# A transpose behind the last value product, a float32r sum over partitions and a last store in halves, in a fused attention and two-layer feed-forward kernel

## The chip, the cores and the metric

The kernel runs on one core of a Trainium2 chip. The metric is the device time of one execution in microseconds (us). Three timed executions of the kernel before took 597.98, 598.2 and 599.4 us, a median of 598.2 us.

## The reference

Causal attention over 2 batches, 12 heads, 448 positions and 64 channels; then a feed-forward layer with a leaky ReLU; then one with an RMS norm ahead and a gate:

```
attn = softmax(mask(q @ k.T / 8)) @ v             # 2 x 12 x 448 x 64
x    = attn, heads side by side                   # 896 x 768
h    = x @ w_in;  x = max(0.01*h, h) @ w_out      # 768 -> 2048 -> 768
rms  = sqrt(mean(x*x, axis=-1) + 1e-6)
xn   = x / rms * rms_g
g    = xn @ w_gate                                # 768 -> 1536
out  = (g*sigmoid(g) * (xn @ w_val)) @ w_out2     # 1536 -> 768
```

The weights and rms_g come as 64-bit floats and are decoded on the chip.

## The kernel before

Activations lie transposed, features on the 128 partitions and tokens in the free dimension, 448 per batch. Every large product is made of float32r operands in two parts, a high part (the value rounded to float32r) and a low part (what is left): high times high, low times high and high times low are accumulated in one PSUM bank, three matmuls of 128x448 where one would stand. The program has five stages on TensorE (PE).

1. **Attention**, some 97 us. A hand-written order (the string ORDER) interleaves 12 pairs of heads with the first weight pieces. A pair's probabilities are transposed on PE (line 365, plain float32 transposes against the identity `ident`), and its value product (line 385) multiplies them with v in plain float32, two heads side by side, each with 64 columns of weights. Steps y0 and y1 (lines 402 to 404) already compute two blocks of the first layer for batch 0. The last PE step of ORDER is x11, the last value product.
2. **First layer**: `first` (its `prod`, lines 152 to 154) does the same two blocks for batch 1, then 14 blocks at line 507 (36 matmuls each).
3. **Second product** (lines 523 to 525), six output blocks of 96 matmuls. ACT and DVE square each block and add the squares up in `ss`, 128 partitions by 896 tokens (lines 530 to 534).
4. **Gate and value products**, 12 blocks, each two weight pieces times two batches through `prod`, 18 matmuls each. In the first block, behind the gate product of each batch, `inv_rms` (line 541) sums `ss` over partitions: one plain float32 matmul of `ones` (128x128) with 448 columns (line 543). DVE and ACT make 1/rms of it (lines 545 to 552) and write it over `ss`; `gated` (line 558) multiplies it in.
5. **Last product** (lines 597 to 599), for two halves of 384 output columns, seven blocks of 128 tokens: 36 matmuls of 128x384 per block, a copy out of PSUM into `o`, on ACT for even blocks (line 608) and on DVE for odd ones (line 610), and a store of 192 KB issued by SP (line 611).

The weight pieces of stages 2 to 5 are loaded by SP and decoded by ACT and DVE (lines 103 to 139) one piece ahead of PE. PSUM is eight banks: four in the pool psS, three in psT (tag t, which the transposes of attention use too), one in psX; behind attention `bank()` hands them out in turn. Behind attention each engine's order is the order of a list scheduler, but for PE it is close to that of the code.

Of the kernel before, what the change touches and what calls it, by code (L numbers as in the profile page):

```python
# [6 lines left out]
F32 = mybir.dt.float32  # L7
F32R = mybir.dt.float32r
# [7 lines left out]
P = 128  # L16
B, H, S, D = 2, 12, 448, 64
# [3 lines left out]
Q = 64  # L21
T = B * S
# [49 lines left out]
def fused_kernel(tc, q, k, v, w_in, w_out, w_gate, w_val, w_out2, rms_g, out):  # L72
    nc = tc.nc
    PE, ACT, DVE, POOL, SP = nc.tensor, nc.scalar, nc.vector, nc.gpsimd, nc.sync

    with ExitStack() as top:
        const = top.enter_context(tc.tile_pool(name="const", bufs=1))
        wst = top.enter_context(tc.tile_pool(name="wst", bufs=2))
        slA = top.enter_context(tc.tile_pool(name="slA", bufs=1))
        mw = top.enter_context(tc.tile_pool(name="mw", bufs=2))  # L80

        ones = const.tile([P, P], F32, name="ones")
        POOL.memset(ones, 1.0)
        pace = const.tile([P, 2 * P], mybir.dt.bfloat16, name="pace")
        DVE.memset(pace, 1.0)
        rg = const.tile([P, KC], F32, name="rg")
# [59 lines left out]
        def rest(lo, x, hi, eng=None):  # L146
            (eng or DVE).tensor_tensor(out=lo, in0=x, in1=hi.bitcast(F32), op=ALU.subtract)
# [17 lines left out]
        HALF = DM // 2  # L165
# [24 lines left out]
        def piece(n, ahead=AHEAD):  # L190
            while len(ready) <= min(n + ahead, len(pieces) - 1):
                src, k_, m_, nm = pieces[len(ready)]
                hl = (None, None)
                if nm:
                    sl = slot(nm)
                    hl = (sl[:, 0, :k_ * m_], sl[:, 1, :k_ * m_])
                steps, parts = begun.pop(len(ready), None) or decode(src, k_, m_, *hl)
                for step in steps:
                    step()
                ready.append(parts())  # L200
            return ready[n]
# [35 lines left out]
        def attention(att, psS, psT, psX, ident, mask, mask_tail, keep_busy):  # L237
# [211 lines left out]
            for name in ORDER.split():  # L449
                name, _, eng = name.partition("@")  # L450
# [4 lines left out]
            assert all(name[0] == "l" and int(name[2:]) in PLAIN for name in do), do.keys()  # L455
            SP.dma_start(out=rg, in_=rms_g.rearrange("(c p) -> p c", p=P))
            ready.extend(L["w", f] for f in range(EARLY))

        psS = top.enter_context(tc.tile_pool(name="psS", bufs=4, space=PSUM))
        psT = top.enter_context(tc.tile_pool(name="psT", bufs=3, space=PSUM))  # L460
        psX = top.enter_context(tc.tile_pool(name="psX", bufs=1, space=PSUM))
        with tc.manual_schedule(), tc.tile_pool(name="att", bufs=2) as att:
            ident = att.tile([P, P], F32, name="ident", bufs=1)
            make_identity(nc, ident)
            mask = att.tile([P, 3 * P], F32, name="mask", bufs=1)
            mask_tail = att.tile([P, S], F32, name="mask_tail", bufs=1)
            for t, rows in ((mask, P), (mask_tail, Q)):
                POOL.memset(t, 0.0)
                for lo in range(0, P, rows):
                    tri = t[lo:lo + rows, -rows:]  # L470
                    POOL.affine_select(out=tri, in_=tri, pattern=[[-1, rows]], compare_op=ALU.is_ge, fill=-BIG,
                                       base=0, channel_multiplier=1)

            warm = psX.tile([P, 512], F32, tag="x", name="warm")

            def keep_busy(n):
                for _ in range(n):
                    PE.matmul(warm[:, :2 * P], pace[:, :P], pace, start=True, stop=True)

            keep_busy(14)  # L480
            attention(att, psS, psT, psX, ident, mask, mask_tail, keep_busy)
# [4 lines left out]
        mx = top.enter_context(tc.tile_pool(name="mx", bufs=2))  # L486
# [3 lines left out]
        def bank(n=S):  # L490
            pool, tag = ((psT, "t"), (psT, "t"), (psT, "t"), (psS, "s"),
                         (psS, "s"), (psS, "s"), (psS, "s"), (psX, "x"))[cnt[0] % 8]
            cnt[0] += 1
            return pool.tile([P, 512], F32, tag=tag, name="mm")[:, :n]
# [6 lines left out]
        for f in range(EARLY, NF1):  # L501
            wt, pss = piece(f), [bank() for _ in range(B)]
            for kk in range(KC):
                wh, wl = wt[kk]
                for w, part in ((wh, 0), (wh, 1), (wl, 0)):
                    for b in range(B):
                        PE.matmul(pss[b], w, cols(xT[kk], b)[part], start=kk + part == 0 and w is wh,  # L507
                                  stop=kk == KC - 1 and w is wl)
# [6 lines left out]
        ss = one.tile([P, T], F32, name="ss")  # L515
        for m in range(KC):
# [9 lines left out]
            for b in range(B):  # L526
                ps = pss[b]
                sq = ss[:, b * S:(b + 1) * S]
# [10 lines left out]


        def inv_rms(b):
            ps = bank()
            PE.matmul(ps, ones, ss[:, b * S:(b + 1) * S], start=True, stop=True)
            ms = mx.tile([P, S], F32, tag="t0", name="ms")
            DVE.tensor_scalar(out=ms, in0=ps, scalar1=1.0 / DM, scalar2=1e-6, op0=ALU.mult, op1=ALU.add)
            r0 = mw.tile([P, S], F32, tag="t1", name="r0")
            ACT.activation(out=r0, in_=ms, func=AF.Abs_reciprocal_sqrt)

            e = mx.tile([P, S], F32, tag="t2", name="e")
            ACT.activation(out=e, in_=r0, func=AF.Square)  # L550
            DVE.scalar_tensor_tensor(out=e, in0=e, scalar=-0.5, in1=ms, op0=ALU.mult, op1=ALU.mult)
            DVE.scalar_tensor_tensor(out=ss[:, b * S:(b + 1) * S], in0=e, scalar=1.5, in1=r0,
                                     op0=ALU.add, op1=ALU.mult)
# [17 lines left out]
        for f in range(NF2):  # L571
            banks = [[None] * B, [None] * B]
            for half in range(2):
                wt = piece(at_gate[f, half])
                for b in range(B):
                    ps = banks[half][b] = bank()
                    prod(ps, [(wt[kk], cols(x2[kk], b)) for kk in range(KC)])
                    if f == 0 and half == 0:
                        inv_rms(b)
                    if half:  # L580
                        gated(f, b, banks[0][b], ps)


        for nh in range(2):
            w2 = []
            for i in range(6):
                w2 += piece(at_w2[nh, i], 0)
            open_ = {}

            def rows(t, lo, hi):  # L590
                if t not in open_:
                    open_[t] = bank(HALF)
                ps = open_[t]
                for f in range(lo, hi):
                    th = tT[f][:, 0, t * P:(t + 1) * P]
                    tl = tT[f][:, 1, t * P:(t + 1) * P]
                    PE.matmul(ps, th, w2[f][0], start=(f == 0), stop=False)  # L597
                    PE.matmul(ps, th, w2[f][1], start=False, stop=False)  # L598
                    PE.matmul(ps, tl, w2[f][0], start=False, stop=(f == NF2 - 1))  # L599

            rows(0, 0, 8)
            rows(1, 0, 8)
            for t in range(T // P):
                rows(t, 8 if t < 2 else 0, NF2)
                ps = open_[t]
                o = mx.tile([P, HALF], F32, tag="t0", name="o")
                if t % 2 == 0:
                    ACT.copy(out=o, in_=ps)
                else:
                    DVE.tensor_copy(out=o, in_=ps)  # L610
                SP.dma_start(out=out[t * P:(t + 1) * P, nh * HALF:(nh + 1) * HALF], in_=o)


# [28 lines left out]
```

## Time and profile before

| | |
|---|---|
| the three timed executions | 597.98, 598.2, 599.4 us; median 598.2 |
| the profiled execution | 597.57 us |
| its span, first to last instruction | 595.7 us |
| PE busy | 588.1 us of the span (99%) |
| DVE, ACT, POOL busy | 386.3 (65%), 264.1 (44%), 48.2 us (8%) |
| attention / stages 2 and 3 with the first gate product / rest of 4 / stage 5 | to 97.4 / to 331.8 / to 504.8 / to 595.7 us |

The profiled execution lies 0.63 us below the median of the timed ones. The time outside its span is 597.57 - 595.7 = 1.9 us. In the profile a matmul's duration is longer than the distance to the next one's start, since matmuls are pipelined: what counts for PE's time is the distance from start to start. A plain float32 matmul is recorded as two, a float32r one or a transpose as one.

### The profile page before, as it was taken

To read this page: it belongs to the slowest core of one execution; us is meant where nothing else is said; L and a number is where in the kernel's file an instruction comes from. 1 tells how busy PE (TensorE), PEld (TensorE's weight loads), DVE (VectorE), ACT (ScalarE), POOL (GpSimd) and SP (SyncE) were. 2 spreads that over 40 slices of the span, in tenths; PEclk is the share of its full clock that TensorE was granted. 3 is DMA by queue.
4 is the path that set the end of the run, shared out by engine and by line. 5 is a ranking of instruction groups with operands and counts; after the bars stand their busy time and mean duration, and the time that the engine had idled before them with its cause. 6 is when DMAs were issued, how large, how long until landed. Compare 5 with 4: busy or idle time off the path is not lost.

```text
span 595.7 us, 8511 instructions
## 1 busy us (share of the span) xinstructions
PE 588.1 (99%) x3266; PEld 532.3 (89%) x3266; DVE 386.3 (65%) x704; ACT 264.1 (44%) x516; POOL 48.2 (8%) x105
## 2 busy tenths in 40 slices
PE   8999999999999999999999999999999999999997
PEld 5778877999999999999999899999999999999997
DVE  4989986866666555555655898797797796850000
ACT  5989883444444434323432753443444444320000
POOL 3644650000000000000000000000000000000000
PEclk9999999999999999999999999999999999999999
DMA  5575451533333323323333334343353352621001
GB/s 130 119 164 115 95 153 45 168 111 107 107 104 105 107 94 116 106 90 114 116 106 107 107 125 140 106 160 111 110 157 120 120 145 88 185 80 41 28 26 41
DMA packets 83992, 65.04 MB, mean 109 GB/s; under 512 B 36080, under 2 KB 80880, under 8 KB 83952
## 3 DMA queue, kind: packets, MB, share of 16 engines
q1 hardware_dynamic: 83024, 64.27, 36.7%
q8 instruction: 26, 0.43, 0.3%
q10 hardware_dynamic: 928, 0.23, 0.2%
q14 instruction: 14, 0.11, 0.1%
HBM read 61.74 MB, written 2.75 MB: 108 GB/s over the span
## 4 chain that ended last, share of the span: by engine, by line
PE 94%; POOL 1%; ACT 1%; DMA 1%; SPq 1%; DVE 1%; issue 0%; POOLq 0%; ACTq 0%; DVEq 0%
PE mm L507 17%; PE mm L152 10%; PE mm L153 10%; PE mm L154 10%; PE mm L524 7%; PE mm L525 7%; PE mm L523 7%; PE mm L599 5%; PE mm L598 5%; PE mm L597 5%; PE s L328 3%; PE pt L365 3%; PE x L385 3%; PE qk L288 1%; POOL p L358 1%; ACT p L345 1%
## 5 line engine op out<-in xcount | busy, mean ns | idle before, releaser
L152 PE MATMUL mm<-a,hi 128*128 128x448 f32 x300 | 110.4, 368 | 0.0
L154 PE MATMUL mm<-a,hi 128*128 128x448 f32 x300 | 109.6, 365 | 0.0
L153 PE MATMUL mm<-a,lo 128*128 128x448 f32 x300 | 109.6, 365 | 0.0
L133 ACT CAST hi<-we 128x768 fp32r<-128x768 f32 (+1 forms) x58 | 47.2, 815 | 137.1 <-PE mm L507 53.6
L139 DVE TENSOR_TENSOR lo<-we,hi 128x768 fp32r<-128x768 f32 (+1 forms) x60 | 55.8, 929 | 66.2 <-ACT hi L133 66.0
L122 DVE SCALAR_TENSOR_TENSOR we<-we,ws 128x768 int32<-128x768 int32 (+1 forms) x70 | 65.6, 937 | 28.9 <-ACT we L111 26.9
L507 PE MATMUL mm<-a,hi 128*128 128x448 f32 x336 | 83.0, 368 | 0.0
L111 ACT ACTIVATE we<-raw 128x768 f32<-128x768 f32 (+1 forms) x67 | 59.5, 888 | 38.1 <-DVE lo L139 24.3
L507 PEld LDWEIGHTS mm<-a,hi 128*128 128x128 f32 x336 | 63.1, 188 | 6.3
L126 DVE SCALAR_TENSOR_TENSOR we<-raw,we 128x768 int32<-128x768 int32 (+1 forms) x70 | 65.3, 933 | 1.4
L523 PE MATMUL mm<-b,hi 128*128 128x448 f32 x168 | 61.8, 368 | 0.0
L524 PE MATMUL mm<-b,hi 128*128 128x448 f32 x168 | 61.8, 368 | 0.0
L525 PE MATMUL mm<-b,lo 128*128 128x448 f32 x168 | 61.8, 368 | 0.0
L152 PEld LDWEIGHTS mm<-a,hi 128*128 128x128 f32 x300 | 56.4, 188 | 4.9 <-issue 0.4
L153 PEld LDWEIGHTS mm<-a,lo 128*128 128x128 f32 x300 | 56.4, 188 | 4.9 <-issue 0.4
L154 PEld LDWEIGHTS mm<-a,hi 128*128 128x128 f32 x300 | 56.4, 188 | 4.5
L507 PE MATMUL mm<-a,lo 128*128 128x448 f32 x168 | 48.3, 368 | 0.0
L345 ACT ACTIVATE p<-p,st 128x128 f32<-128x128 f32 (+3 forms) x84 | 44.0, 531 | 2.7 <-DVE st L336 2.5
L118 DVE TENSOR_SCALAR ws<-raw 128x768 int32<-128x768 uint32 (+1 forms) x70 | 37.9, 542 | 5.2 <-DMA raw<-in_moe_w_out_dram 2.6
L358 POOL TENSOR_SCALAR p<-p,st 128x384 f32<-128x384 f32 (+3 forms) x76 | 38.5, 528 | 30.0 <-DVE st L354 19.0
L610 DVE COPY o<-mm 128x384 f32<-128x384 f32 x6 | 3.3, 556 | 53.2 <-PE mm L599 53.2
L523 PEld LDWEIGHTS mm<-b,hi 128*128 128x128 f32 x168 | 31.6, 188 | 3.2
(125 smaller groups left out, 931.7 us busy)
## 6 DMA issues: line engine op xcount, KB each, us to landing
raw<-in_moe_w_out_dram SPq DMA_DIRECT2D x24, 768.0 KB, 4.3
raw<-in_moe_w_in_dram SPq DMA_DIRECT2D x16, 768.0 KB, 4.7
raw<-in_moe_w_gate_dram SPq DMA_DIRECT2D x12, 768.0 KB, 4.3
raw<-in_moe_w_val_dram SPq DMA_DIRECT2D x12, 768.0 KB, 4.3
raw<-in_moe_w_out_dram SPq DMA_DIRECT2D x6, 512.0 KB, 3.4
n<-in_k_dram SPq DMA_DIRECT2D x24, 112.0 KB, 2.8
out_dram<-o SPq DMA_DIRECT2D x14, 192.0 KB, 1.9
vn<-in_v_dram SPq DMA_DIRECT2D x24, 96.0 KB, 2.4
```

Source lines behind the costliest of these rows:

```text
L111: ACT.activation(out=out, in_=src, func=AF.Copy, scale=2.0 ** -112)
L122: DVE.scalar_tensor_tensor(out=L["e"], in0=L["e"], scalar=3, in1=L["s"], op0=ALU.logical_shift_left, op1=ALU.bitwise_or)
L126: DVE.scalar_tensor_tensor(out=L["e"], in0=L["w"][:, :, 1], scalar=-0x80000000, in1=L["e"], op0=ALU.bitwise_and, op1=ALU.bitwise_or)
L139: DVE.tensor_tensor(out=L["lo"], in0=L["e"].bitcast(F32), in1=L["hi"].bitcast(F32), op=ALU.subtract)
L152: PE.matmul(ps, wh, ah, start=(i == 0), stop=False)
L153: PE.matmul(ps, wl, ah, start=False, stop=False)
L154: PE.matmul(ps, wh, al, start=False, stop=(i == n - 1))
L345: ACT.activation(out=pr, in_=pr, func=AF.Exp, scale=-1.0, bias=st[:, 0, m:m + 1], accum_out=st[:, 1, m:m + 1])
L507: PE.matmul(pss[b], w, cols(xT[kk], b)[part], start=kk + part == 0 and w is wh, stop=kk == KC - 1 and w is wl)
L523: PE.matmul(pss[b], wh, ah, start=(f == 0), stop=False)
L524: PE.matmul(pss[b], wh, al, start=False, stop=False)
L525: PE.matmul(pss[b], wl, ah, start=False, stop=(f == NF1 - 1))
```

## The change

Three edits. `ones` becomes a float32r tile, so that `inv_rms` can split `ss` into a high part `sh` (copied by ACT) and a low part `sl` (subtracted on DVE, through `rest`, line 147) and accumulate two float32r matmuls in place of a plain float32 one. Behind the whole of ORDER stands one transpose of 64 rows of the identity into a fresh psT bank, whose result nobody reads. The last of the 14 output blocks is copied and stored in two halves of 192 columns: ACT copies and stores the first, DVE copies the second and SP stores it.

```diff
-        ones = const.tile([P, P], F32, name="ones")
-        POOL.memset(ones, 1.0)
+        ones = const.tile([P, P], F32R, name="ones")
+        POOL.memset(ones.bitcast(F32), 1.0)
...
             ready.extend(L["w", f] for f in range(EARLY))
+            PE.transpose(psT.tile([P, 512], F32, tag="t", name="pt")[:, :Q], ident[:Q], ident[:Q, :Q])
...
         def inv_rms(b):
-            ps = bank()
-            PE.matmul(ps, ones, ss[:, b * S:(b + 1) * S], start=True, stop=True)
+            ps, sq = bank(), ss[:, b * S:(b + 1) * S]
+            sh = mw.tile([P, S], F32R, tag="t1", name="sh")
+            ACT.copy(out=sh, in_=sq)
+            sl = mx.tile([P, S], F32R, tag="t2", name="sl")
+            rest(sl, sq, sh)
+            PE.matmul(ps, ones, sh, start=True, stop=False)
+            PE.matmul(ps, ones, sl, start=False, stop=True)
...
                 o = mx.tile([P, HALF], F32, tag="t0", name="o")
-                if t % 2 == 0:
-                    ACT.copy(out=o, in_=ps)
-                else:
-                    DVE.tensor_copy(out=o, in_=ps)
-                SP.dma_start(out=out[t * P:(t + 1) * P, nh * HALF:(nh + 1) * HALF], in_=o)
+                cuts = [0, HALF // 2, HALF] if (nh, t) == (1, T // P - 1) else [0, HALF]
+                for i, (lo, hi) in enumerate(zip(cuts, cuts[1:])):
+                    if (t + i) % 2 == 0:
+                        ACT.copy(out=o[:, lo:hi], in_=ps[:, lo:hi])
+                    else:
+                        DVE.tensor_copy(out=o[:, lo:hi], in_=ps[:, lo:hi])
+                    (ACT if i == 0 and len(cuts) > 2 else SP).dma_start(
+                        out=out[t * P:(t + 1) * P, nh * HALF + lo:nh * HALF + hi], in_=o[:, lo:hi])
```

The order of the instructions on PE at the end of attention, as one piece of the difference (x is the value product's bank, pt the transpose's, mm a bank of the first layer, a_72 the first slice of attention's output, hi and lo the parts of a weight piece):

```order
 L385 MATMUL x<-pT,vn_129 64x192 x2
 L385 MATMUL x<-pT,vn_129 64x64 x2
+L458 MATMUL pt<-ident 128x64
 L152 MATMUL mm<-a_72,hi 128x448
 L153 MATMUL mm<-a_72,lo 128x448
```

Nothing moved here but the added transpose, which stands between the last value product and the first float32r matmul of stage 2.

PE at the first `inv_rms`, in stage 4, with the semaphores that a row waits for (each is named for the engine that counts it up, or for a DMA queue), before:

```order
L154 MATMUL mm<-a_2462,hi 128x448 [waits DVE_49]
L543 MATMUL mm<-ss,ones 128x448
L152 MATMUL mm<-a_2457,hi 128x448
L153 MATMUL mm<-a_2457,lo 128x448
L154 MATMUL mm<-a_2457,hi 128x448
```

and with the change:

```order
L154 MATMUL mm<-a_2464,hi 128x448 [waits DVE_49]
L548 MATMUL mm<-sh,ones 128x448 [waits Activation_49]
L152 MATMUL mm<-a_2459,hi 128x448
L549 MATMUL mm<-sl,ones 128x448 [waits DVE_49]
L153 MATMUL mm<-a_2459,lo 128x448
L154 MATMUL mm<-a_2459,hi 128x448
```

The two new matmuls wait, one for ACT and one for DVE, and the next product's first matmul stands between them. DVE at the same place with the change (lo, we and ws belong to the decoding of a weight piece; L551 reads the sum):

```order
L538 SCALAR_TENSOR_TENSOR a_2464<-mm,rg,a_2464 128x448 [waits Activation_49]
L139 TENSOR_TENSOR lo<-we,hi 128x768 [waits PE_49,Activation_49]
L147 TENSOR_TENSOR sl<-ss,sh 128x448 [waits Activation_49]
L122 SCALAR_TENSOR_TENSOR we<-we,ws 128x768 [waits Activation_49]
L551 TENSOR_SCALAR ms<-mm 128x448 [waits PE_49]
```

The low part sl stands behind a weight piece's L139; on ACT its high part sh (L545) stands behind that piece's L133 and ahead of the next piece's L111.

DVE at the end of the program with the change:

```order
L618 COPY o<-mm 128x384 [waits DMAHW4_49,DVE_49,PE_49]
L618 COPY o<-mm 128x384 [waits DMAHW3_49,DMAHW5_49,DMAHW0_49,DMAHW7_49,PE_49,Activation_49]
L618 COPY o<-mm 128x384 [waits DMAHW1_49,DVE_49,PE_49]
L618 COPY o<-mm 128x384 [waits DMAHW3_49,DVE_49,PE_49]
L618 COPY o<-mm 128x192 [waits DMAHW4_49,DMAHW2_49,DMAHW6_49,DMAHW0_49,Activation_49]
```

The added half copy waits for ACT, not for PE: the ACT instruction that it waits for is the copy of the first half, which writes the same tile and reads the same bank.

## Rows read from the trace of the kernel before

**Rows 1.** The page: granted clock by slice, and the chain that ended last.

```profile
PEclk9999999999999999999999999999999999999999
PE 94%; POOL 1%; ACT 1%; DMA 1%; SPq 1%; DVE 1%; issue 0%; POOLq 0%; ACTq 0%; DVEq 0%
```

**Rows 2.** Two stretches: us, PE busy (matmuls) and other engines, clock, DMA.

```profile
97.70:331.84 234.14, 234.14 (x1134) 212.68 (x1133) 141.85 (x194) 92.84 (x152) 0.00 (x0) 1.00 0.35 112
337.20:504.80 167.60, 167.60 (x829) 155.35 (x828) 139.21 (x203) 74.52 (x105) 0.00 (x0) 1.00 0.41 126
```

**Rows 3.** Timeline of PE, end of attention: start us, us, engine, line, operation.

```profile
96.84 0.61 PE L385 MATMUL x<-pT,vn 128*64 128x192 f32 x8
97.38 0.47 PE L152 MATMUL mm<-a,hi 128*128 128x448 f32 x1
97.70 0.36 PE L153 MATMUL mm<-a,lo 128*128 128x448 f32 x1
```

**Rows 4.** Timeline of PE, float32r behind transposes (qk is one's bank).

```profile
70.73 0.27 PE L291 MATMUL qk<-ident,end 128*128 128x128 f32 x1
70.76 0.45 PE L402 MATMUL mm<-a,hi 128*128 128x448 f32 x1
71.05 0.37 PE L403 MATMUL mm<-a,lo 128*128 128x448 f32 x1
...
72.67 0.38 PE L365 MATMUL pt<-ident,p 128*128 128x128 f32 x2
```

**Rows 5.** Timeline, both `inv_rms` on PE: the float32 matmul, the second row behind it.

```profile
331.84 0.92 PE L543 MATMUL mm<-ss,ones 128*128 128x448 f32 x2
...
332.80 0.37 PE L153 MATMUL mm<-a,lo 128*128 128x448 f32 x1
...
336.25 0.91 PE L543 MATMUL mm<-ss,ones 128*128 128x448 f32 x2
...
337.20 0.36 PE L153 MATMUL mm<-a,lo 128*128 128x448 f32 x1
```

**Rows 6.** Timeline, ACT and DVE ahead of the first `inv_rms`.

```profile
329.60 0.85 ACT L133 CAST hi<-we 128x768 fp32r<-128x768 f32 x1
...
330.57 0.94 DVE L139 TENSOR_TENSOR lo<-we,hi 128x768 fp32r<-128x768 f32 x1
...
332.47 0.96 DVE L122 SCALAR_TENSOR_TENSOR we<-we,ws 128x768 int32<-128x768 int32 x1 [0.97 <-ACT we L111]
```

**Rows 7.** Groups by line and shape: busy us, mean ns of one, idle before.

```profile
L378 ACT COPY pT<-pt 128x512 f32<-128x512 f32 x38 | 21.5, 582 | 4.8 <-PE pt L365 4.3
...
L147 DVE TENSOR_TENSOR b<-g,b 128x448 fp32r<-128x448 f32 x28 | 16.3, 622 | 4.8 <-ACT b L219 4.8
...
L219 ACT CAST b<-g 128x448 fp32r<-128x448 f32 x28 | 14.4, 571 | 0.0
...
L378 DVE COPY pT<-pt 128x512 f32<-128x512 f32 x10 | 6.8, 685 | 0.7 <-PE pt L365 0.6
...
L608 ACT COPY o<-mm 128x384 f32<-128x384 f32 x8 | 3.8, 479 | 62.0 <-PE mm L599 62.0
...
L610 DVE COPY o<-mm 128x384 f32<-128x384 f32 x6 | 3.3, 556 | 53.2 <-PE mm L599 53.2
```

**Rows 8.** Timeline, end of the program.

```profile
592.43 0.48 ACT L608 COPY o<-mm 128x384 f32<-128x384 f32 x1 [12.01 <-PE mm L599]
592.93 0.33 SPq L611 DMA_DIRECT2D out_dram<-o  x1
```

**Rows 9.** DMA issues: count, KB each, median us to landing.

```profile
out_dram<-o SPq DMA_DIRECT2D x14, 192.0 KB, 1.9
vn<-in_v_dram SPq DMA_DIRECT2D x24, 96.0 KB, 2.4
...
vn<-in_v_dram SPq DMA_DIRECT2D x12, 32.0 KB, 2.4
```

**Rows 10.** Waits: who waited for whom, us in total, times, longest.

```profile
ACT hi L133 <- PE mm L507: 53.6, 14, 4.2
```

## The prediction

> **What bounds the kernel.** I read the page first: the chain that ended last is PE for 94% of the span, and the granted clock is full in every slice, the 2.4 GHz level [rows 1]. Behind attention nothing else ends a wait for long, so the time there is a number of matmuls times the distance from one start to the next. The second view, busy time by stretch, gives that distance, and it is not the same everywhere [rows 2]. From 97.70 to 331.84 us PE is never idle and starts 1133 matmuls of 128x448 (the row counts one more, still in flight at its left edge): 234.14 / 1133 = 0.2067 us each. From 337.20 to 504.80 us it starts 827 of the same shape and type (the row counts one in flight at either edge): 167.60 / 827 = 0.2027 us. The clock is 1.00 in both, the lines of `prod` stand in both, and neither has idle time. The same form runs 4.0 ns slower in the first stretch than in the second.
>
> The third view, PE's timeline, shows what stands at the borders. The slow stretch begins straight behind the last value product, whose matmuls use 64 columns of weights in pairs [rows 3]. It ends at the plain float32 matmul of `inv_rms` [rows 5]: the gate product's first 18 matmuls ahead of it still go at 0.2067, those behind it at 0.2027. A third place decides: in attention a run of eight float32r matmuls of 128x448, entered from transposes, takes from 71.05 to 72.67 us [rows 4]. That is 1.62 / 8 = 0.2025 us, where the slow pace would need 1.65. So I read the pace as something that PE keeps from how it entered a run of float32r matmuls: slow out of the value product, fast out of a transpose or a 128-column float32 matmul.
>
> **The transpose.** It stands exactly at the slow entry. If it acts as the transposes of rows 4 do, all 1133 distances fall to 0.2027: 1133 x 0.0040 = 4.53 us off PE, which is the path. Nothing behind it has to keep up that does not already: ACT's high part of the next weight piece waited for PE in 14 of the 14 blocks of line 507, 3.8 us a time [rows 10], and a block of 36 matmuls shortens by only 0.14. Its own cost: in rows 4 the float32r matmul starts 0.03 us behind the last transpose and the next one 0.29 behind that, against 0.32 between the first two in rows 3. That makes it nothing at the least and about 0.1 at the most; I take +0.05. Its bank is an extra turn in psT, free since the last transposes.
>
> **The sum over partitions.** From the start of the float32 matmul to the start of the second row behind it are 0.96 and 0.95 us [rows 5]. One of the 0.2027 in it belongs to the float32r matmul, so each sum costs 0.75. Now it is two float32r matmuls, 2 x 0.2027 = 0.41, and 0.34 is saved, twice: -0.69. The new operands are covered, but barely. ACT makes sh (571 ns for a cast of this width, rows 7) behind the high part that ends at 330.45, so by 331.02 [rows 6]. DVE makes sl (622 ns) behind L139, which ends at 331.51, so at 332.13, inside an idle 0.97 us. PE, at the fast pace behind the second product, comes to the sl matmul at 331.84 - 22 x 0.004 + 2 x 0.203 = 332.16. The scheduler's extra matmul between the two gives just this much, so I add +0.05 for a wait. Behind the wait stands the rest of the second batch's product. At the second sum I count no wait of its own; one of this size is within the range. What ACT and DVE do later for it (two casts and two subtractions, 2.4 us in all) lies beside the 36 value matmuls that follow, 36 x 0.2027 = 7.3 us.
>
> **The last store.** This looks like a saving and the order says it is not. Before, ACT's copy starts at 592.43 and SP issues 0.50 us later [rows 8]. Now DVE's half waits for ACT's half. From 384 to 512 columns ACT's copies grow from 479 to 582 ns and DVE's from 556 to 685 [rows 7], so 192 columns take some 325 and 362 ns: 0.325 + 0.03 + 0.362 + 0.02 = 0.74, and the last issue comes 0.24 us later. What the half as large store gives back is not in the trace: loads of 96 and of 32 KB both land after 2.4 us, so nothing; in proportion to bytes, half of 1.9, 0.95 [rows 9]. So between -0.71 and +0.24. The loads are the nearer rows, as they change the size alone, but the stores go the other way; I take 0.14 back and +0.10 for the edit.
>
> **The sum.** -4.53 + 0.05 - 0.69 + 0.05 + 0.10 = -5.02 us: 597.57 - 5.0 = 592.6 us for the profiled execution. The median of the runs shown lies 0.63 above it, so I forecast 593.2 us, 0.84% less. A measurement of this kernel can tell about 0.3%, 1.8 us, from no change.
>
> **Rivals**, each on the same scale (598.2 before).
>
> The pace outlives the transpose. The added one covers only 64 of the 128 rows, while every transpose that I see ahead of fast runs covers 112 or 128. If it leaves the slow pace standing, the change takes away the only thing that ended it, the float32 matmul: the two float32r matmuls are of the form that runs in either pace, and the 846 gate and value matmuls behind the first sum go at 0.2067 too. That is +3.38, with -0.68 for the sums and +0.2 for the rest: 601.1 us, slower; up to 2.0 more if the last stage's 504 matmuls, which ran at 173 ns each, were slower as well by 4 ns. It decides at one point: whether the second start behind the transpose lies 0.203 or 0.207 behind the first, and stays there. For it: the difference in rows. Against it: the entry is then from another instruction than a value product.
>
> The pace belongs to the stage and not to its entry, to something in operands or buffers of the first stretch that I don't see. Then the transpose does nothing and the gate stage stays fast: -0.69 + 0.2 = -0.5, 597.7 us. Against it speaks that `prod` runs at both paces on the same operands on either side of the sum. [...]
>
> The transpose helps, and the wait at the sl matmul enters the run anew and slowly. Then 3.38 is given back: -4.53 + 3.38 - 0.68 + 0.2 = -1.6, 596.6 us.
>
> **Chances.** Fast throughout, 593.2 us: 0.74. Slow throughout, 601.1: 0.11. No effect of the transpose, 597.7: 0.09. Half given back, 596.6: 0.06. Faster by over 0.3% (below 596.4) is the first case alone, 0.74; within 0.3% are the two small savings, 0.15; slower 0.11. The range begins at 592.0: the forecast less the best end of the store, 0.8, and the uncertainty of the median. It must reach the half-way case to hold eight in ten, so it ends at 596.8; the likeliest case alone lies within 592.0 and 594.0.
>
> **What would show it.** Right: behind 97.7 us the 1133 float32r matmuls take 229.6 us instead of 234.1; the gate stage keeps 0.2027; the two sums take 0.41 us each with no wait above 0.1; the last issue comes 0.74 us behind the start of ACT's copy and DVE's copy starts as ACT's ends. Wrong: a distance of 0.2067 behind the transpose, or behind 332 us; a sum that costs 0.7 because PE stood for sl; DVE's and ACT's half copies side by side.

## The result, and the profile after

The changed kernel took 593.1 us (median of four executions, 592.66 to 593.52) beside 598.13 us for the kernel before on the same chip: ratio 0.9911, 95% interval 0.9894 to 0.9928. The forecast was 593.2. The profiled execution took 592.95 us.

First the page: the span with its instructions, the busy times, and the chain that ended last.

```profile
span 591.2 us, 8521 instructions
...
PE 584.7 (99%) x3267; PEld 534.0 (90%) x3267; DVE 387.6 (66%) x707; ACT 265.2 (45%) x518; POOL 48.3 (8%) x105
...
PE 95%; POOL 1%; ACT 1%; DVE 1%; DMA 1%; issue 0%; ACTq 0%; POOLq 0%
```

Nothing here tells what happened: PE bounds the kernel as before [rows 1] and is 99% busy as before. The stretches do, in the columns of [rows 2].

```profile
98.34:327.96 229.62, 229.62 (x1134) 212.78 (x1133) 141.78 (x195) 93.24 (x153) 0.00 (x0) 1.00 0.37 114
333.75:500.30 166.55, 166.55 (x823) 154.34 (x822) 139.23 (x203) 74.54 (x104) 0.00 (x0) 1.00 0.41 126
```

The first stretch holds the same 1133 distances as in [rows 2]. They took 234.14 us and now take 229.62: 0.2027 us each in place of 0.2067. The second stretch keeps its pace (166.55 / 0.2027 = 822 distances). The clock is 1.00 in both. PE's timeline at the entry, with the transpose in the first row:

```profile
97.83 0.27 PE L458 MATMUL pt<-ident 64*128 64x64 f32 x1
98.04 0.47 PE L152 MATMUL mm<-a,hi 128*128 128x448 f32 x1
98.34 0.36 PE L153 MATMUL mm<-a,lo 128*128 128x448 f32 x1
```

The rows are rounded to 0.01 us; by the trace's nanoseconds the first float32r matmul starts 201 ns behind the transpose, and the second 306 ns behind the first, close to the 313 ns of [rows 3]. PE at the first sum:

```profile
327.96 0.36 PE L548 MATMUL mm<-sh,ones 128*128 128x448 f32 x1
328.16 0.37 PE L152 MATMUL mm<-a,hi 128*128 128x448 f32 x1
328.37 0.47 PE L549 MATMUL mm<-sl,ones 128*128 128x448 f32 x1
328.69 0.37 PE L153 MATMUL mm<-a,lo 128*128 128x448 f32 x1
```

ACT and DVE there, and the weight load of the sl matmul (PEld is the part of PE that loads weights ahead of a matmul):

```profile
326.53 0.60 ACT L545 CAST sh<-ss 128x448 fp32r<-128x448 f32 x1
...
327.70 0.62 DVE L147 TENSOR_TENSOR sl<-ss,sh 128x448 fp32r<-128x448 f32 x1
...
328.37 0.19 PEld L549 LDWEIGHTS mm<-sl,ones 128*128 128x128 f32 x1 [0.22 <-DVE sl L147]
```

DVE's low part ends at 328.32, and the weight load of the sl matmul, for which PEld stood idle for 0.22 us, starts at 328.37 together with the matmul. The matmul itself comes almost in time, but it takes 0.11 us longer than its neighbours (0.47 instead of 0.36) and the next start lies 0.31 behind it instead of 0.20. The whole sum costs 0.41 + 0.11, against 0.75 for the float32 matmul that it replaces. The end of the program, in the order of time:

```profile
587.53 0.34 PE L605 MATMUL mm<-hi,b 128*128 128x384 f32 x1
...
587.95 0.32 ACT L616 COPY o<-mm 128x192 f32<-128x192 f32 x1 [12.01 <-PE mm L605]
...
588.30 0.37 ACTq L619 DMA_DIRECT2D out_dram<-o  x1
588.30 0.36 DVE L618 COPY o<-mm 128x192 f32<-128x192 f32 x1 [6.08 <-ACT o L616]
588.69 0.33 SPq L619 DMA_DIRECT2D out_dram<-o  x1
```

The DMA issues to the output (count, KB each, median us to landing):

```profile
out_dram<-o SPq DMA_DIRECT2D x13, 192.0 KB, 1.9
out_dram<-o ACTq DMA_DIRECT2D x1, 96.0 KB, 1.7
out_dram<-o SPq DMA_DIRECT2D x1, 96.0 KB, 1.6
```

DVE's half copy starts as ACT's ends. The last issue stands 0.74 us behind the start of ACT's copy (before 0.50, rows 8), and the halves land in 1.7 and 1.6 us instead of 1.9.

Where the span's 4.52 us went (595.69 to 591.17; starts of the same instructions in both traces, in nanoseconds and then rounded):

| part | before | after | difference | forecast |
|---|---|---|---|---|
| up to the last value product (nothing changed there) | 95.50 | 95.95 | +0.45 | 0 |
| value product to the first float32r matmul | 1.88 | 2.08 | +0.20 | +0.05 |
| the first distance behind it | 0.31 | 0.31 | -0.01 | 0 |
| 1133 distances | 234.15 | 229.62 | -4.53 | -4.53 |
| first sum to the last product | 172.95 | 172.38 | -0.57 | -0.64 |
| last product to its last matmul | 87.21 | 87.19 | -0.02 | 0 |
| last matmul to the end | 3.68 | 3.63 | -0.05 | +0.10 |

Without the first row, in which the programs do not differ, -4.97 us stand against the -5.02 of the sum.

### The profile page after: what moved, and what is told of

The parts are those of the page before. It is cut to its first block, busy times and chain, and to the rows that moved or that the text cites. A ratio compares the mean times of both kernels' runs of the same rounds, so it can differ in the third digit from the quotient of the medians.

```text
span 591.2 us, 8521 instructions
## 1 busy us (share of the span) xinstructions
PE 584.7 (99%) x3267; PEld 534.0 (90%) x3267; DVE 387.6 (66%) x707; ACT 265.2 (45%) x518; POOL 48.3 (8%) x105
## 4 chain that ended last, share of the span: by engine, by line
PE 95%; POOL 1%; ACT 1%; DVE 1%; DMA 1%; issue 0%; ACTq 0%; POOLq 0%
PE mm L508 17%; PE mm L152 10%; PE mm L153 10%; PE mm L154 10%; PE mm L525 7%; PE mm L526 7%; PE mm L524 7%; PE mm L605 5%; PE mm L604 5%; PE mm L603 5%; PE s L328 3%; PE pt L365 3%; PE x L385 3%; PE qk L288 2%; POOL p L358 1%; ACT p L345 1%
## 5 line engine op out<-in xcount | busy, mean ns | idle before, releaser
L133 ACT CAST hi<-we 128x768 fp32r<-128x768 f32 (+1 forms) x58 | 47.4, 818 | 131.8 <-PE mm L508 51.3
L139 DVE TENSOR_TENSOR lo<-we,hi 128x768 fp32r<-128x768 f32 (+1 forms) x60 | 55.8, 930 | 62.9 <-ACT hi L133 62.9
L111 ACT ACTIVATE we<-raw 128x768 f32<-128x768 f32 (+1 forms) x67 | 59.4, 887 | 37.9 <-DVE lo L139 23.4
L618 DVE COPY o<-mm 128x384 f32<-128x384 f32 (+1 forms) x7 | 3.7, 528 | 59.4 <-PE mm L605 53.3
L336 DVE CUSTOM_DVE_ANT_0 p<-s,mask 128x128 f32<-128x128 f32 (+2 forms) x72 | 27.5, 416 | 11.1 <-PE s L314 8.2
```

The costliest lines, as they stand in the source:

```text
L111: ACT.activation(out=out, in_=src, func=AF.Copy, scale=2.0 ** -112)
L139: DVE.tensor_tensor(out=L["lo"], in0=L["e"].bitcast(F32), in1=L["hi"].bitcast(F32), op=ALU.subtract)
```

## The experiments

The result fits the sum. The reason given for it was still to be tried: that PE keeps a pace from how it entered a run of float32r matmuls, slow out of the value product, fast out of a transpose or a float32 matmul of 128 columns. One view serves for all runs: three stretches without idle time, 110 to 200 us in the first layer, 220 to 320 in the second product, 345 to 495 in the gate and value products. Columns are those of [rows 2]; the number to read is the count of PE's matmuls. At 0.2067 us the stretches hold 435, 484 and 726 distances, at 0.2027 444, 493 and 740, and the rows count one to three more, those in flight at an edge included. So **437 or 438, 485 or 486, 728 is the slow pace, and 445 or 446, 495 or 496, 742 the fast one.** The starts in nanoseconds show the same two paces without any mean: at the slow one every distance is 206 or 207 ns, and each matmul starts 204 or 205 ns behind the start of its own weight load; at the fast one the distances go round in fives, of about 199, 207, 202, 203 and 202 ns, any five in a row taking 1013 or 1014 ns, and the weight load lies 195 to 205 ns ahead (the two kernels below, all six stretches). The kernel before:

```profile
110.00:200.00 90.00, 90.00 (x438) 81.74 (x437) 56.59 (x76) 42.03 (x73) 0.00 (x0) 1.00 0.37 111
220.00:320.00 100.00, 100.00 (x485) 90.83 (x485) 56.70 (x79) 33.39 (x50) 0.00 (x0) 1.00 0.34 108
345.00:495.00 150.00, 150.00 (x742) 139.04 (x741) 126.21 (x184) 64.68 (x91) 0.00 (x0) 1.00 0.42 132
```

and with the change:

```profile
110.00:200.00 90.00, 90.00 (x446) 83.40 (x445) 57.13 (x77) 42.33 (x73) 0.00 (x0) 1.00 0.37 113
220.00:320.00 100.00, 100.00 (x495) 92.67 (x494) 56.05 (x78) 33.91 (x51) 0.00 (x0) 1.00 0.36 116
345.00:495.00 150.00, 150.00 (x742) 139.00 (x741) 125.00 (x181) 63.71 (x89) 0.00 (x0) 1.00 0.42 132
```

### One edit at a time

**The transpose alone**, in the kernel before:

```diff
             ready.extend(L["w", f] for f in range(EARLY))
+            PE.transpose(psT.tile([P, 512], F32, tag="t", name="pt")[:, :Q], ident[:Q], ident[:Q, :Q])
```

> The transpose alone, on the kernel before. Theory (PE keeps a pace from how a run of float32r matmuls was entered): all 1133 distances from 98 us on are 0.2027 us, the plain float32 sums stay at 0.75 us each, 598.1 - 4.53 + 0.2 for the transpose = 593.8 us. Rival (the pace belongs to the stage, and the gain came from the sums or the store): distances stay 0.2067, 598.3 us.

593.37 us (593.18 to 593.75), ratio 0.9926 (0.9911 to 0.9941).

```profile
110.00:200.00 90.00, 90.00 (x446) 83.41 (x445) 56.63 (x76) 42.58 (x74) 0.00 (x0) 1.00 0.38 114
```

The transpose alone brings all of the gain that can be told from zero.

**The sums alone**: the edits to `ones` and `inv_rms`, in the kernel before, no transpose.

> The float32r sums alone, on the kernel before: no transpose, so the run is entered from the value product, and no plain float32 matmul ends it. Theory: 0.2067 us from 97.7 us through the first sum and on through the gate and value products to the last product, 846 x 0.004 = +3.38, less 0.6 for the sums: 600.9 us, slower than before though it does less on PE. Rival (the pace belongs to the stage): the gate stage stays at 0.2027, 597.5 us.

Median 600.45 us, ratio 1.0026 (1.0009 to 1.0043), in two groups: seven of ten executions took 600.2 to 602.4 us and three 597.0 to 597.4. The groups' medians lie 3.2 us apart, and 846 gate and value matmuls at 4.0 ns more each are 3.4. The profiled execution is one of the seven:

```profile
345.00:495.00 150.00, 150.00 (x728) 136.25 (x727) 125.53 (x182) 63.99 (x91) 0.00 (x0) 1.00 0.41 127
```

The slow pace, which the float32 matmul had ended, now goes on through both float32r sums. So this edit, which saves 0.6 us of PE's work, makes the kernel slower in seven executions of ten when it stands alone. Of the three quicker executions no trace was taken; that they ran this stretch at the fast pace is read from their time alone.

**The halves alone**: the last store's edit, in the kernel before.

> The last store in halves alone, on the kernel before. Theory: copies one behind the other, last issue 0.24 us later, landing some 0.3 us sooner: no change, 598.1 us within 0.3. Rival (halves save): 597.6 us, with the span behind the last matmul's start shorter than 3.6 us.

597.93 us, ratio 1.0007 (0.9997 to 1.0016): no difference. The end of its timeline:

```profile
592.62 0.32 ACT L610 COPY o<-mm 128x192 f32<-128x192 f32 x1 [12.01 <-PE mm L599]
...
592.97 0.36 DVE L612 COPY o<-mm 128x192 f32<-128x192 f32 x1 [6.08 <-ACT o L610]
...
593.35 0.33 SPq L613 DMA_DIRECT2D out_dram<-o  x1
```

Again the copies stand one behind the other, and from the last matmul's start to the end of the span are 3.63 us, against 3.68 before.

### Is it the entry, and what about it?

**The transpose in the middle**: the same line between the stage of line 507 and the second product, in the kernel before (the identity moved to a pool that lives on).

> The kernel before with the transpose between line 507's stage and the second product instead of behind the value product (its identity lies in another pool). Theory: 0.2067 us for the 539 distances ahead of it, 0.2027 for the 594 behind it: 594 x 0.004 = 2.38 less, some 0.3 more for the transpose in mid-stream, 596.0 us. Rival (the pace belongs to the stage, or is settled once at the end of attention): 0.2067 up to the first sum, 598.4 us.

595.96 us (595.76 to 596.15), ratio 0.9968 (0.9956 to 0.998).

```profile
110.00:200.00 90.00, 90.00 (x437) 81.77 (x436) 56.80 (x77) 42.20 (x73) 0.00 (x0) 1.00 0.37 111
220.00:320.00 100.00, 100.00 (x496) 92.69 (x495) 57.81 (x81) 33.28 (x50) 0.00 (x0) 1.00 0.34 109
```

Slow ahead of it, fast behind it: the pace turns where the transpose stands, whatever stage that is.

**A pause in place of the transpose**: the first 18 float32r matmuls, still entered from the value product, then one float32r matmul of the same shape that has to wait for ACT.

```diff
+            first(0, 1, ready[0], psT.tile([P, 512], F32, tag="t", name="mm")[:, :S])
+            PE.matmul(psT.tile([P, 512], F32, tag="t", name="late")[:, :S], ready[0][0][0], cols(gT[0], 1)[0],
+                      start=True, stop=True)
...
-        for f in range(EARLY):
+        for f in range(1, EARLY):
```

> The kernel before (no transpose, plain float32 sums) with a pause of PE and nothing else: behind the first 18 float32r matmuls of the first layer stands one more of the same form whose operand ACT makes from their result, so that PE waits some 1.4 us; it multiplies for nobody. Theory one (what clears the slow pace is a matmul of another form that uses all 128 columns): 0.2067 us on both sides of the pause, 598.0 + 1.6 = 599.6 us. Theory two (the pace is how PE settled into the steady stream, and any break lets it settle anew): 0.2067 ahead of the pause, 0.2027 behind it, 1115 x 0.004 = 4.46 less, 595.1 us.

595.15 us, ratio 0.9962 (0.9945 to 0.9979); one execution of ten took 599.49 us.

```profile
101.34 0.37 PE L154 MATMUL mm<-a,hi 128*128 128x448 f32 x1
102.93 0.47 PE L459 MATMUL late<-a,hi 128*128 128x448 f32 x1 [1.23 <-ACT a L219]
```

```profile
110.00:200.00 90.00, 90.00 (x446) 83.52 (x445) 57.04 (x77) 42.03 (x73) 0.00 (x0) 1.00 0.36 111
```

There is no foreign instruction here, only 1.23 us in which PE stood. The distances are 0.207 ahead of it and 0.2027 behind it.

**A bfloat16 matmul in place of the transpose**, with the change otherwise whole (`pace` is a bfloat16 tile set once):

```diff
-            PE.transpose(psT.tile([P, 512], F32, tag="t", name="pt")[:, :Q], ident[:Q], ident[:Q, :Q])
+            PE.matmul(psT.tile([P, 512], F32, tag="t", name="pt")[:, :Q], pace[:, :P], pace[:, :Q], start=True, stop=True)
```

> The kernel after with a bf16 matmul (128 columns of weights, 64 columns of data) in place of the transpose. If any 128-column matmul of another form clears the slow pace: 0.2027 from 98 us on, 593.1 us. If it must be a float32 form or a transpose: 0.2067 to the last product, 600.5 us, or some 597.2 in executions in which the wait in the sums breaks the stream.

595.67 us (594.27 to 595.95), ratio 0.9957 (0.9942 to 0.9972): neither expectation. Of the four executions one, at 594.27, lies between the two paces' times.

```profile
220.00:320.00 100.00, 100.00 (x495) 92.76 (x494) 56.27 (x79) 34.15 (x51) 0.00 (x0) 1.00 0.36 116
345.00:495.00 150.00, 150.00 (x728) 136.31 (x727) 124.80 (x180) 62.95 (x88) 0.00 (x0) 1.00 0.40 127
```

Fast up to the sums, slow behind them. This is the third rival of the prediction, in which the sums give back 3.4 us, though in another kernel. PE waited for sl here as it did with the change (0.30 us from the sl matmul to the next start), and in this trace the steady 0.207 begins right behind that matmul.

**A transpose with 64 columns of weights**, with the change otherwise whole: all 128 rows of the identity, but 64 columns as in the value product.

```diff
-            PE.transpose(psT.tile([P, 512], F32, tag="t", name="pt")[:, :Q], ident[:Q], ident[:Q, :Q])
+            PE.transpose(psT.tile([P, 512], F32, tag="t", name="pt")[:Q, :P], ident[:, :Q], ident)
```

> The kernel after with a transpose that uses 64 columns of weights (and all 128 rows) in place of 64 rows. If 128 columns clear the slow pace: it stays at 0.2067 to the last product, 600.5 us (or some 597.2 where the sums break it). If the transpose as such clears it, or any matmul that is not a value product: 0.2027, 593.1 us.

592.44 us (592.33 to 593.14), ratio 0.991 (0.9896 to 0.9925), the lowest median of all, though the interval is nearly that of the change. At the entry and by stretch:

```profile
97.51 0.30 PE L458 MATMUL pt<-ident 128*64 128x128 f32 x1
97.56 0.45 PE L152 MATMUL mm<-a,hi 128*128 128x448 f32 x1
```

```profile
110.00:200.00 90.00, 90.00 (x446) 83.51 (x445) 56.64 (x76) 42.47 (x74) 0.00 (x0) 1.00 0.38 115
345.00:495.00 150.00, 150.00 (x742) 139.16 (x741) 124.40 (x180) 63.41 (x89) 0.00 (x0) 1.00 0.42 132
```

It does not take 128 columns. And the float32r matmul starts 0.05 us behind this transpose, not 0.20.

**The value product's own form in the middle**, with the change otherwise whole:

```diff
+        col = psT.tile([P, 512], F32, tag="t", name="pt")
+        for j in range(2):
+            PE.matmul(col[Q * j:Q * j + Q, :Q], ident[:, :Q], ident[:, :Q], start=True, stop=True)
         x2 = [mid.tile([P, T], F32, name="x2") for i in range(NP)]
```

> The kernel after (transpose kept) with a pair of plain float32 matmuls of 64 columns of weights, two heads' form of the value product, between line 508's stage and the second product; nobody reads their result. If the form of the last matmul before the run sets the pace: 0.2027 up to the pair and 0.2067 behind it to the last product, 1439 x 0.004 = +5.76 and some 0.4 for the pair, 599.3 us (596.0 where the sums break the stream). If the value product was slow for another reason than its form: 0.2027 throughout, 593.5 us.

593.43 us (593.11 to 596.54), ratio 0.993 (0.9907 to 0.9953).

```profile
220.00:320.00 100.00, 100.00 (x495) 92.77 (x494) 56.04 (x78) 33.79 (x51) 0.00 (x0) 1.00 0.36 116
```

Fast behind a pair of plain float32 matmuls with 64 columns of weights; the one execution at 596.54 lies where a turn at the sums would put it. So the form of the last matmuls ahead of the run is not enough to make the pace slow, and the theory as the prediction put it falls.

### Do the sums need their wait?

What was left: does the 0.1 us wait at the sl matmul turn the pace in the bfloat16 kernel, or the sums themselves? In three runs both `inv_rms` stand behind both gate products, so that sh and sl are long done:

```diff
-                    if f == 0 and half == 0:
-                        inv_rms(b)
+                if f == 0 and half == 0:
+                    for b in range(B):
+                        inv_rms(b)
```

With the 64-column transpose:

> The kernel after with the 64-column transpose, and with both sums issued behind the gate products of both batches instead of each behind its own, so that their operands are ready long before PE comes to them. Theory (a break lets PE settle anew at one of two paces; without a break it keeps the one it has): no matmul of the sums waits, 0.2027 from 98 us to the last product in every execution, 592.3 us, all executions within 0.5. Rival (the sums themselves disturb the pace): some executions at 595.7.

595.95 us (595.4 to 597.69, ten executions), ratio 0.9965 (0.9953 to 0.9977). PE at the second sum, and by stretch:

```profile
335.60 0.36 PE L548 MATMUL mm<-sh,ones 128*128 128x448 f32 x1
...
336.21 0.37 PE L549 MATMUL mm<-sl,ones 128*128 128x448 f32 x1
336.41 0.37 PE L154 MATMUL mm<-a,hi 128*128 128x448 f32 x1
336.62 0.37 PE L152 MATMUL mm<-a,hi 128*128 128x448 f32 x1
```

```profile
220.00:320.00 100.00, 100.00 (x496) 92.66 (x495) 56.03 (x78) 33.76 (x51) 0.00 (x0) 1.00 0.36 116
...
345.00:495.00 150.00, 150.00 (x728) 136.24 (x727) 126.46 (x182) 63.77 (x89) 0.00 (x0) 1.00 0.42 132
```

No matmul waited, and the pace turned from fast to slow at this sl matmul, in the middle of a run: the theory's 592.3 us did not come. With the bfloat16 matmul:

> The kernel after with the bf16 matmul in place of the transpose, and the sums issued late as above. Theory: fast from 98 us on, and nothing breaks the run: 0.2027 to the last product in every execution, 592.3 us. Rival (a run entered from a bf16 matmul is only half settled, and any other matmul tips it): slow behind the sums again, 595.7.

596.06 us (595.58 to 596.88, nine executions), ratio 0.996 (0.9948 to 0.9972).

```profile
345.00:495.00 150.00, 150.00 (x728) 136.33 (x727) 126.57 (x183) 64.02 (x90) 0.00 (x0) 1.00 0.43 132
```

Slow again, here from the first sum on. And with no entry edit:

> The kernel before with the float32r sums and no transpose, as in the second run, but the sums issued late as above. Theory: the slow pace from the value product on is broken by nothing, 0.2067 to the last product in every execution, 600.4 us and none at 597. Rival (the sums, not the wait in them, changed the pace in some executions): both times again.

600.8 us (600.72 to 601.63, four executions), ratio 1.0043 (1.0026 to 1.0061).

```profile
345.00:495.00 150.00, 150.00 (x728) 136.25 (x727) 127.02 (x186) 65.37 (x93) 0.00 (x0) 1.00 0.41 128
```

Slow throughout, and none near 597 us. So float32r sums that wait for nothing can end the fast pace, by the times in all 19 executions of the two kernels that come to them fast, and did not end the slow one in any of four. Not each sum does it: the one that turned the pace was the second with the 64-column transpose and the first with the bfloat16 matmul, and with the change the second sum, which waits for nothing either, left it standing. In the kernels with the sums in their first place, where PE waits 0.1 us for the first sl, the fast pace came out in all executions of the change (four) and of the 64-column transpose (four), by their times in four of five of the kernel with the added pair, but not in the profiled one of the bfloat16 kernel, where the slow pace begins right behind the same wait. So the short wait goes with a fast pace more often than not, but it is not enough, and that it helps at all is not shown: the late sums differ in their place as well.

**A pause at the entry itself**: in the kernel before, one float32r matmul behind the last value product that waits for DVE's copy of that product.

```diff
+            PE.matmul(psT.tile([P, 512], F32, tag="t", name="late")[:, :S], ready[0][0][0], cols(xT[NP - 1], 1)[0],
+                      start=True, stop=True)
```

> The kernel before (no transpose, plain float32 sums) with one float32r matmul behind the last value product whose operand DVE makes from that product, so that PE enters the run some 0.9 us later; it multiplies for nobody. If the value product as such leaves PE slow: 0.2067 up to the first sum, 598.0 + 1.1 = 599.1 us. If the slow pace comes of entering straight behind it and a pause is enough: 0.2027, 598.0 + 1.1 - 4.53 = 594.6 us.

594.42 us (594.32 to 594.54), ratio 0.9934 (0.9917 to 0.995).

```profile
98.42 0.47 PE L458 MATMUL late<-a,hi 128*128 128x448 f32 x1 [0.73 <-DVE a L393]
98.73 0.37 PE L152 MATMUL mm<-a,hi 128*128 128x448 f32 x1
```

```profile
110.00:200.00 90.00, 90.00 (x446) 83.50 (x445) 56.90 (x77) 42.15 (x73) 0.00 (x0) 1.00 0.37 111
```

The instruction ahead is still the value product; 0.73 us of standing between them is enough. Against the kernel before in its own series of runs it gains 3.74 us (598.16 to 594.42), the transpose alone 4.64 (598.01 to 593.37). Of the 0.90 between them the traces show 0.80 at the entry: from the start of the value product to the second matmul of the first layer 3.19 us instead of 2.39.

## Why the prediction was right, and where not

**The first edit did what was forecast, and its size was exact.** A pace is set where the run is entered, and the transpose set the fast one. The 1133 distances fell from 0.2067 to 0.2027 us, -4.53. The transpose alone gave 593.37, and the place of a transpose moved the turn. The Trainium skill (TensorE: Matmul & The Clock Gate, Back-to-back issue gap) gives N / 2.4 + 2.5 ns, 189 ns at 448 columns, as the gap of an isolated matmul at full clock, and says that in a stream of weight loads and matmuls both of them set the spacing. In the traces here no stretch of the first layer or behind it ran its 448 columns at 0.189: both paces are longer, 0.2027 and 0.2067 us.

**"Slow out of the value product, fast out of a transpose or a 128-column float32 matmul" was too narrow.** What the runs show is two settled paces of one stream, and that the stream takes one of them when it starts anew. Straight out of the value product it was slow in all six traces of that entry. Behind a transpose of either form, a bfloat16 matmul, a pair of 64-column float32 matmuls or a pause of 0.7 us or more it was fast in every trace, and by the times in nearly every execution (nine of ten for the pause). Nor does PE keep the pace from the entry alone: with the late sums it turned in the middle of a run. Why a start settles at the one or the other stays open: the runs vary what stands ahead of it, and the distances right at the start don't tell the two apart (304 and 313 to 315 ns ahead of slow runs, 284 to 311 ahead of fast ones).

**The rivals.** "The pace outlives the transpose" did not come about, but its price is real: take the transpose away and the new sums let the slow pace through, and the kernel takes 600.45 us, near its 601.1. "The transpose helps, and the sl matmul enters slowly" was given 0.06. With the change it did not happen in four executions; with a bfloat16 matmul in the transpose's place it did, at 595.67, near its 596.6. Its reason is not settled: in that trace the slow pace begins right behind the wait for sl, but the late sums turn the pace without any wait. The chance was low for how close the case lay. That the change itself came through its sums at the fast pace is in part luck: nothing in the prediction told its entry from one that differs in a single matmul and lost the pace there. "The pace belongs to the stage" fell with the transpose in the middle.

**The sums** saved 0.57 of the forecast 0.64: the wait for sl was 0.11 and not 0.05. In the measured time this is not to be seen: the change lies 0.3 us below the transpose alone, inside both intervals.

**The two terms that were mis-sized** cancel, which is luck. The transpose's own cost was forecast at 0.05, with 0.1 as the most that seemed possible from rows 4, and measured 0.20. The 64-column form costs 0.05: the bound had come from transposes of 128 rows and 128 columns of data, and the added one has 64 of each; which of the two makes the difference is not shown. The store was forecast at +0.10 and measured -0.05: the copies stand in series as foreseen, and the last issue is 0.24 later, but half a store lands 0.3 us sooner, not 0.14.

**The agreement to 0.1 us** (593.1 against 593.2) is luck as well. The profiled execution was forecast at 592.6 and took 592.95, mostly for the 0.45 us that attention took longer in that execution, and the median lay 0.15 us above it and not 0.63.

**On the signs foreseen:** 229.6 us for the 1133 distances, 0.2027 in the gate stage, the last issue 0.74 behind the copy, DVE's copy behind ACT's, all as written. The first sum's wait, at 0.11, lies just above the 0.1 that was named.

## What to carry to other kernels

Where PE is 99% busy, compare the distance from start to start of equal matmuls stretch by stretch: a busy share cannot show a stream that goes 2% slower. If one stretch is slower, an instruction of 0.05 to 0.20 us or a pause at its entry is a cheap trial. An edit in another place, here a cheaper sum, can turn the pace of the matmuls behind it, so read the distances anew after each edit, and take several executions.

## What the hardware showed that was not expected

- The pace of float32r matmuls can change in the middle of a run in which nothing waits: from 0.203 to 0.207 us at one sl matmul, and then so for 700 matmuls and more, at a granted clock of 1.00.
- A pause of 0.73 us on PE pays: it costs 1.00 us with its matmul (3.19 instead of 2.19 us from the value product to the second matmul of the first layer), brings 4.5 us over the matmuls behind it, and the kernel gains 3.7.
- The last product, float32r with 384 columns, showed one pace only: from 560 to 580 us the kernel before and the one with late sums and no transpose both count 117 matmuls (20 / 0.173 = 116), every distance 173 or 174 ns, although the first comes from the fast pace and the second from the slow one.
- A transpose of 64 rows of float32 holds the next float32r matmul up by 0.20 us, one of 128 rows with 64 columns by 0.05, and a bfloat16 matmul with 64 columns of data by 0.04.
- A store of 96 KB landed in 1.6 to 1.7 us where one of 192 KB took 1.9, while loads of 96 and 32 KB took the same 2.4 [rows 9].
